# Attention and two mixture-of-experts layers: the table is entered one list later, the logits come in column fourths, and the second layer's rows are gathered before the earlier output

## The chip, the cores and the metric

One core of one Trainium2 chip runs the whole program in one launch. The metric is the device time of one execution in microseconds; it was 559.38 us (median of three runs).

## What is computed

Three parts follow each other; the first layer's capacity is 288 rows for an expert.

```python
# attention: q, k, v are 2 x 8 x 576 x 64, mask by blocks of 64
scores = where(block_i >= block_j, q @ k.T / 8, -1e9)
x = (softmax(scores) @ v)                         # then 1152 tokens x 512
# first layer: the best of 8 experts, at most 288 tokens each
e = argmax(x @ w_gate); gate = softmax(x @ w_gate)[e]
x = gate * (relu(x_e @ w1[e]) @ w2[e])            # 512 -> 1024 -> 512, 0 where not kept
# second layer: noisy choice of two of 8 experts
noisy = x @ w_gate + log1p(exp(x @ w_noise)) * noise
top2 = the two largest of noisy; weights = softmax over these two
out = sum over both of weight * (relu(x @ w1[e]) @ w2[e])
```

## The kernel before, in words

PE is TensorE, DVE VectorE, ACT ScalarE, POOL GpSimd, SP SyncE. The attention takes the first 141 us, the first layer's eight experts e0 to e7 about 141 to 334, the second layer the rest.

**Products.** A product in fp32 is made of three matmuls (`mm3`, L197 to L200): high part by high part, high by low, low by high. SP loads the weights as they are (`raw`), ACT makes the high part (L167), DVE the low one (L170). Tokens are handled in blocks of 128 rows, which indirect DMAs on POOL fetch: `xr` from x_d in the first layer (L1441), `g` in the second (L1418). PE transposes them (L1015), ACT and DVE split them (L1018, L1021).

**Order.** All work between the attention and the end is put into lists. A list is a `Flow` (L929): operations with an engine, a guessed duration and dependencies; `run` draws an order for every engine from weights and a random seed in `PAR` (L30). Each engine then goes through its own order and waits on semaphores. There is a list for each expert and arm, and at its end a branch. In the first layer the program holds two arms for each expert from e1 on: a short list (SMALL, one block of 128 rows or fewer) and a long one (LARGE, two blocks, and behind it a third block where the expert has more than 256 rows). In these data e1 to e4 take the short list, e5 to e7 the long one, and e6 also the third block. The list that carries over to the second layer is KNOWN (expert 0 of the second layer, from L1739), then comes `arm(e)` for e = 1 to 7 (kind SECOND), and `rest(e)` where an expert has over 256 rows.

**post (L1219).** When the first layer has finished a block of rows (`px`), `post` finds for each row its two experts of the second layer and the places in their lists. It runs in the next list: the last block of an expert is posted in the list of the next expert; in LARGE and in the third block another post runs within the list. There are twelve. Its steps:

- POOL: `place` (L1228 to L1233) and `send` (L1236), the scatter of the rows into x_d.
- PE transposes px (L1243), ACT copies it (`x2t`, L1247), and four matmuls make the logits (L1252): the rows are the stationary side, 16 columns of `wcat` (gate and noise) stream.
- ACT and DVE: exp, log, noise, the maximum and its index (L1256 to L1277), and M, the choice as ones and zeros (L1281).
- PE: the rank matmuls (L1286, L1288) count the rows of each expert; DVE picks the places (L1315 to L1325) and makes the weights v (L1303 to L1310).
- DVE: cells C (L1335), slots S (L1329) and C by v (L1340); PE: the table matmul (L1345, two of 144 columns); DVE adds the result to the table T (L1349).

T says which rows each expert of the second layer gathers. The table is the last matmul of most lists.

**Second layer.** `arm(e)` issues on POOL, in this order: the two fetches `prev` of what the output holds (L1577), then the next expert's gathers and the third block's (L1418), and at its end the scatters of the result (L1586), which have added the fetched rows (L1583). The fetches stand ahead of the list, where the loop at the end of the kernel calls them:

```python
for e in range(1, E):
    for blk in range(2):
        prev(G[e, blk][1], blk)
    arm(e)
```

Of the kernel before, what the change touches and what calls it, by code (L numbers as in the profile page):

```python
# [29 lines left out]
PAR = [dict(P=0.05, A=0.2, V=0.3, G=0.2, fit=0.52, late=0.548, dma=2.7, when=5.0, split=0, prep=1.8, post=1.85, last=2.5, seed=8387, noise=0.2),  # L30
       dict(P=0.2, A=0.2, V=0.2, G=0.1, fit=0, late=0.32, dma=2.44, when=10.0, split=6.3, prep=0, post=0.3, last=8.0, seed=5942, noise=0.2),
# [15 lines left out]
def attention_moe_moe2(ctx, tc, q, k, v, wg1, w1a, w2a, cap, wg2, wn2, noise, w1b, w2b, out):  # L47
    nc = tc.nc
# [44 lines left out]
    wcat = consts.tile([128, KD, 16], F32, name="wcat")  # L93
# [203 lines left out]
    with ExitStack() as actx:  # L297
# [69 lines left out]
        def gates(b):  # L367
            if b == B:
                nc.sync.dma_start(out=wcat[:, :, 0:8], in_=wg2.rearrange("(k p) e -> p k e", p=128))
# [556 lines left out]

    nc.vector.tensor_scalar(cum, ioe, float(NG), None, op0=OP.mult)
# [5 lines left out]
    class Flow:  # L933
# [4 lines left out]
        def __init__(self, kind=OTHER):  # L938
            self.kind, self.par, self.table = kind, PAR[kind], None
# [279 lines left out]
    def post(F, pd, n=128, deps=(), ranks=None, last=False, early=()):  # L1219
# [5 lines left out]
        def place():  # L1225
            fl = tl["fl"] = small.tile([128, 3], F32, name="fl")
            v = tl["v"] = small.tile([128, 2, 2], F32, name="v")
# [90 lines left out]
        def dest():  # L1318
            d = tl["di"] = small.tile([128, 3, 2], I32, name="di")
# [7 lines left out]
        def slots():  # L1327
            S2 = tl["S2"] = small.tile([128, 2, 128], F32, name="S2", bufs=1)
            nc.vector.tensor_tensor(S2[:n], tl["di"][:n, 1, :, None].to_broadcast([n, 2, 128]),  # L1329
                                    fslot[:n, None, :].to_broadcast([n, 2, 128]), op=OP.is_equal)  # L1330

        def cells():
            g = [n, 2, 8 * NG]
            C1 = tl["C1"] = small.tile([128, 2, 8 * NG], F32, name="C1", bufs=1)
            nc.vector.tensor_tensor(C1[:n], tl["di"][:n, 2, :, None].to_broadcast(g), iog[:n, None, :].to_broadcast(g), op=OP.is_equal)  # L1335

        def filled():
            g = [n, 2, 2, 8 * NG]
            C2 = tl["C2"] = small.tile([128, 2, 2, 8 * NG], F32, name="C2", bufs=1)
            nc.vector.tensor_tensor(C2[:n], tl["C1"][:n, :, None, :].to_broadcast(g), tl["v"][:n, :, :, None].to_broadcast(g), op=OP.mult)  # L1340

        def table(bank):
            tl["T"] = bank[:, 0:16 * NG]
            for j in range(2):
                nc.tensor.matmul(tl["T"], tl["S2"][:n, j], tl["C2"][:n, j].rearrange("p a g -> p (a g)"), start=(j == 0), stop=(j == 1))  # L1345

        def enter():
            c = T2[:, :, :, 0:NG]
            nc.vector.tensor_tensor(c, tl["T"].rearrange("p (a e g) -> p a e g", a=2, e=8), c, op=OP.add)  # L1349
# [25 lines left out]
        c = V(dest, [c])  # L1375
        c = V(parts, [c], 0.15)
        s2 = V(slots, [c, F.table], 0.33)
        c2 = V(cells, [c, F.table], 0.2)
        c2 = V(filled, [c2, w], 0.36)
# [436 lines left out]
```

## Time and profile before

| | |
|---|---|
| median of three runs | 559.38 us (557.72 to 559.82) |
| the profiled execution | 557.14 us, span 555.5 |
| PE busy | 517.0 us (93%) |
| DVE busy | 378.9 us (68%) |
| ACT busy | 294.1 us (53%) |
| POOL busy | 138.4 us (25%) |
| mean granted TensorE clock | 0.992 |
| DMA | 99.17 MB, mean 179 GB/s |

The profiled execution's own time is 1.6 us longer than its span; the median of the runs is 2.2 us above it. A busy share is an average over stages. Every view gives times from the start of the span. In a timeline, the bracket behind a row is the idle time of that engine before it and what ended it; rows start before their forerunner has ended where matmuls overlap, so the step between two of them is the difference of their starts.

### The profile page before, as it was taken

What the parts mean: (1) busy time and instruction counts of PE and PEld (TensorE: products, weight loads), DVE (VectorE), ACT (ScalarE), POOL (GpSimd) and SP (SyncE); (2) the same over time, 40 slices, a digit from 0 to 9 for tenths busy, and PEclk for the clock granted to TensorE, in tenths of its full rate; (3) what the DMA queues carried; (4) which work ended last, traced back from release to release, by engine and by line L of the source; (5) the groups of instructions that cost most, each with busy time, mean ns of one, the idle gap of its engine ahead of it and who ended that gap; (6) DMA issues with size and microseconds to landing.
All of it is one profiled execution on the core that took longest, in us unless ns stands there. A gap on an engine that the chain in (4) does not pass through costs nothing. (4 is left out here: it accounts for less than half of the span.)

```text
span 555.5 us, 10106 instructions
## 1 busy us (share of the span) xinstructions
PE 517.0 (93%) x3381; PEld 422.8 (76%) x3381; DVE 378.9 (68%) x1008; ACT 294.1 (53%) x580; POOL 138.4 (25%) x225
## 2 busy tenths in 40 slices
PE   3999999999869999999999999989999999969996
PEld 3778777878647776787976967888989886949794
DVE  7899988888548988757674678464848562917441
ACT  5888878871347687544533536252635442716130
POOL 3000000000462234405233133142513132514131
PEclk9999999999999999999999999999999999979999
DMA  6998896423458878754632442638658591545220
GB/s 136 221 240 229 220 230 188 123 77 109 137 176 290 265 240 296 232 189 138 206 133 64 170 137 71 226 125 284 221 205 280 188 327 48 187 180 165 86 66 35
DMA packets 71176, 99.17 MB, mean 179 GB/s; under 512 B 37130, under 2 KB 40586, under 8 KB 71088
## 3 DMA queue, kind: packets, MB, share of 16 engines
q1 hardware_dynamic: 63600, 83.16, 47.6%
q0 software_dynamic: 6432, 14.71, 8.4%
q8 instruction: 39, 0.64, 0.5%
q14 instruction: 49, 0.40, 0.2%
q10 hardware_dynamic: 1056, 0.26, 0.2%
HBM read 87.53 MB, written 12.25 MB: 180 GB/s over the span
## 5 line engine op out<-in xcount | busy, mean ns | idle before, releaser
L170 DVE TENSOR_TENSOR wl<-raw,wh 128x512 fp32r<-128x512 f32 x140 | 91.6, 685 | 12.0 <-ACT wh L167 11.6
L167 ACT ACTIVATE wh<-raw 128x1024 fp32r<-128x1024 f32 x70 | 71.1, 1052 | 20.1 <-PEq L1780 12.5
L170 DVE TENSOR_TENSOR both<-raw,both 128x512 fp32r<-128x512 f32 x100 | 66.0, 684 | 8.9 <-ACT both L167 8.4
L167 ACT ACTIVATE both<-raw 128x1024 fp32r<-128x1024 f32 x50 | 51.3, 1054 | 10.0 <-PEq L1780 8.3
L198 PE MATMUL h<-xh,wh 128*128 128x256 f32 (+1 forms) x184 | 52.9, 287 | 0.5
L199 PE MATMUL h<-xl,wh 128*128 128x256 f32 (+1 forms) x184 | 52.6, 286 | 0.0
L200 PE MATMUL h<-xh,wl 128*128 128x256 f32 (+1 forms) x184 | 52.5, 285 | 0.0
L1018 ACT ACTIVATE xh<-tp 128x512 fp32r<-128x512 f32 (+1 forms) x37 | 19.0, 536 | 59.0 <-PE tp L1015 57.3
L1021 DVE TENSOR_TENSOR xl<-tp,xh 128x512 fp32r<-128x512 f32 (+1 forms) x37 | 21.9, 610 | 35.3 <-ACT xh L1018 35.1
L1145 ACT ACTIVATE hh<-h 128x512 fp32r<-128x512 f32 (+1 forms) x46 | 24.1, 523 | 38.7 <-PE h L200 32.3
L1586 POOL DMA_INDIRECT out_dram<-o,T2i x16 | 18.5, 1156 | 96.9 <-DVE o L1583 94.8
L1148 DVE SCALAR_TENSOR_TENSOR hl<-h,hh 128x512 fp32r<-128x512 f32 (+1 forms) x46 | 27.5, 597 | 22.1 <-ACT hh L1145 18.0
L198 PE MATMUL h<-xh,both 128*128 128x256 f32 (+1 forms) x136 | 39.2, 288 | 2.7 <-DVE hl L1148 1.4
L199 PE MATMUL h<-xl,both 128*128 128x256 f32 (+1 forms) x136 | 39.0, 287 | 0.0
L200 PE MATMUL h<-xh,both 128*128 128x256 f32 (+1 forms) x136 | 38.8, 285 | 0.0
L198 PE MATMUL y<-wh,hh 128*128 128x512 f32 (+1 forms) x94 | 38.3, 407 | 0.0
L200 PE MATMUL y<-wh,hl 128*128 128x512 f32 (+1 forms) x94 | 37.1, 394 | 0.0
L199 PE MATMUL y<-wl,hh 128*128 128x512 f32 (+1 forms) x94 | 36.9, 393 | 0.0
L550 ACT ACTIVATE pt<-s,negmax 128x128 f32<-128x128 f32 (+3 forms) x64 | 33.4, 526 | 6.4 <-DVE negmax L537 5.1
L526 PE MATMUL s<-both 128*128 128x256 f32 (+2 forms) x128 | 33.1, 371 | 3.8 <-ACT both L468 2.5
L198 PEld LDWEIGHTS h<-xh,wh 128*128 128x128 f32 x184 | 34.7, 189 | 2.1 <-issue 1.6
L199 PEld LDWEIGHTS h<-xl,wh 128*128 128x128 f32 x184 | 34.6, 188 | 0.0
(295 smaller groups left out, 1297.9 us busy)
## 6 DMA issues: line engine op xcount, KB each, us to landing
raw<-in_moe_w_dram SPq DMA_DIRECT2D x120, 512.0 KB, 5.1
wf<-in_moe_w_dram SPq DMA_DIRECT2D x8, 512.0 KB, 5.8
out_dram<-zero SPq DMA_DIRECT2D x3, 768.0 KB, 5.5
both<-both SPq DMA_DIRECT2D x14, 160.0 KB, 2.6
raw<-in_q_dram SPq DMA_DIRECT2D x16, 128.0 KB, 4.2
vn<-in_v_dram SPq DMA_DIRECT2D x16, 128.0 KB, 2.6
both<-both SPq DMA_DIRECT2D x14, 144.0 KB, 3.3
raw<-in_k_dram SPq DMA_DIRECT2D x14, 128.0 KB, 4.7
```

What stands on the lines that cost most here:

```text
L167: nc.scalar.activation(h, t, AF.Copy)
L170: (nc.gpsimd if part == 3 else nc.vector).tensor_sub(l[:, c], t[:, c], h[:, c].bitcast(F32))
L198: nc.tensor.matmul(o, sh, mh, start=first, stop=False)
L199: nc.tensor.matmul(o, sh, ml, start=False, stop=False)
L200: nc.tensor.matmul(o, sl, mh, start=False, stop=last)
L526: nc.tensor.matmul(o, w[:, i, h, 128 * t:128 * t + 128], w[:, i + 2, h, 64 * h:64 * h + n], start=(i == 0), stop=(i == 1))
L550: nc.scalar.activation(o, i, AF.Exp, bias=negmax[:, pr, 2 * t + h:2 * t + h + 1], accum_out=ssum[b][:, t, 2 * p + h:2 * p + h + 1])
L1018: nc.scalar.activation(xh[:, :, c0:c0 + n], h["tp"][:, :, :n], AF.Copy)
L1021: nc.vector.tensor_tensor(xl[:, :, c0:c0 + n], h["tp"][:, :, :n], xh[:, :, c0:c0 + n].bitcast(F32), op=OP.subtract)
L1145: nc.scalar.activation(part(hfull[0], g - (KF - 2 * WHOLE) // per) if plain(g) else part(hh, g), of(g), AF.Relu)
L1148: nc.vector.scalar_tensor_tensor(part(hl, g), of(g), 0.0, part(hh, g).bitcast(F32), op0=OP.max, op1=OP.subtract)
L1586: ins = nc.gpsimd.indirect_dma_start(out=out, out_offset=_off(G[key][1][:n, 0:1]), in_=G[key, "o"][:n], in_offset=None, bounds_check=NT - ...
```

## The change

Five things are changed.

1. The steps from S and C to the addition into T leave `post` and become a function `enter`, with one buffer each for v, the places, S and C. A list now begins with the entering of the block that the list before has posted last. Only the posts that another post follows within the same list still enter at once (`now=True`), as does KNOWN's. The buffers begin as zeros, so that the first such entering, in e1's list, adds nothing: a thirteenth table. `place` and the picked places wait until the older ones have been read.
2. The logits: `wcat` is the stationary side, 32 columns (16 of them zero), 128 rows stream, and each of the four parts of the contraction goes to its own 32 partitions of PSUM. ACT copies that, and one matmul with `fold`, four stacked identities, sums the fourths.
3. SMALL and LARGE have other weights and seeds, so their orders are drawn anew.
4. The `prev`s of the second layer become entries of the list, and `to_out` depends on them.
5. Gathers that read T wait for the entering (`z`, `z0`).

```diff
-PAR = [dict(P=0.05, A=0.2, V=0.3, G=0.2, fit=0.52, late=0.548, dma=2.7, when=5.0, split=0, prep=1.8, post=1.85, last=2.5, seed=8387, noise=0.2),
+PAR = [dict(P=0.08, A=0.043, V=0.3693, G=0.1233, fit=0.097, late=0.6606, dma=1.5931, when=5.0, split=0, prep=2.0216, post=0.0021, last=10.4267, seed=4319, noise=0.7048),
...
-    wcat = consts.tile([128, KD, 16], F32, name="wcat")
+    wcat = consts.tile([128, KD, 32], F32, name="wcat")
+    fold = consts.tile([128, 16], F32, name="fold")
...
+    nc.gpsimd.tensor_tensor(fold, ident[:, 0:16], ident[:, 32:48], op=OP.add)
...
+    def enter(F, deps=(), early=(), tail="post"):
...
+        used = [F.table] if F.table else []
+        s2 = F.add("V", 0.33, slots, list(deps[:1]) + used)
+        c = F.add("V", 0.2, cells, list(deps[:1]) + used)
+        c2 = F.add("V", 0.36, filled, [c] + list(deps[1:]) + used)
+        t = F.table = F.add("P", 0.7, table, [s2, c2], take="sm")
+        F.entered = [s2, c2]
+        return F.add("V", 0.22, add, [t] + list(early), frees=t, tail=F.par[tail]), s2
...
         def logit(bank):
-            lg = tl["lg"] = bank[:, 0:16]
+            tl["lb"] = bank
             for kk in range(KD):
-                nc.tensor.matmul(lg[:n], tl["xt"][:, kk, :n], wcat[:, kk, :], start=(kk == 0), stop=(kk == KD - 1))
+                nc.tensor.matmul(bank[32 * kk:32 * kk + 32, 0:n], wcat[:, kk], tl["xt"][:, kk, :n], start=True, stop=True)
+
+        def fourths():
+            lq = tl["lq"] = yT.rearrange("p k n -> p (k n)")[:, 1024:1152]
+            nc.scalar.activation(lq[:, :n], tl["lb"][:, 0:n], AF.Copy)
+
+        def logits():
+            lg = tl["lg"] = tl["lb"][:, 128:144]
+            nc.tensor.matmul(lg[:n], tl["lq"][:, :n], fold, start=True, stop=True)
...
-        f = F.add("G", 0.8, place, deps)
+        f = F.add("G", 0.8, place, list(deps) + F.entered)
...
-        lg = F.add("P", 0.85, logit, [a], take="sm")
-        c = F.add("A", 0.1, ex, [lg])
+        lg = F.add("P", 0.45, logit, [a], take="sm")
+        c = F.add("A", 0.25, fourths, [lg])
+        c = F.add("P", 0.25, logits, [c])
+        c = F.add("A", 0.1, ex, [c])
...
+        if now:
+            z, s2 = enter(F, (c, w), early, "last" if last else "post")
...
-            nxt = post(F, first, last=True)[0] if first is not None else None
+            z = enter(F)[0] if first is not None else None
+            nxt = post(F, first, last=True, now=more)[0] if first is not None else None
...
-                d, _ = rows2(F, (0, 0), 0, 0, tis[0])
+                d, _ = rows2(F, (0, 0), 0, 0, tis[0], deps=[z])
...
-                    post(F, pend[2], deps=r, ranks=nxt)
+                    post(F, pend[2], deps=r, ranks=nxt, now=False)
...
-                _, z, _, tl = post(F, cur)
+                enter(F)
+                _, z, _, tl = post(F, cur, now=False)
...
-        blocks(F, E + e, xT[e % 2], 0, lambda y, blk, p, first: to_out(F, y, (e, blk), blk, p, first), done=done, apart=e + 1 == E)
+        before_ = [F.add("G", 1.04, lambda blk=blk: prev(G[e, blk][1], blk), after=3.5 if e + 1 < E else 0.0) for blk in range(2)]
+        blocks(F, E + e, xT[e % 2], 0, lambda y, blk, p, first: to_out(F, y, (e, blk), blk, p, first, deps=[before_[blk]]), done=done, apart=e + 1 == E)
...
-    d, i = rows2(F, (0, "early"), 0, 1, tis[1], deps=[d])
+    z0 = enter(F)[0]
+    d, i = rows2(F, (0, "early"), 0, 1, tis[1], deps=[d, z0])
...
-        for blk in range(2):
-            prev(G[e, blk][1], blk)
         arm(e)
```

Three places show how the instructions move. Line numbers of the change are its own: L1249 is the table, L1287 the transposes of px, L1296 the fourths, L1304 the fold, L1338 and L1340 the ranks, L1447 the gather, L1608 the prev, L1617 the scatter.

**POOL, the second layer's list of one expert**, before:

```order
L1577 DMA px_1732<-out_dram,T2i 128x512
L1577 DMA px_1733<-out_dram,T2i 128x512
L1418 DMA g_1740<-x_d,T2i 128x524
L1418 DMA g_1741<-x_d,T2i 128x524
L1418 DMA g_1742<-x_d,T2i 32x524
L1386 TENSOR_LOAD cnt_92
L1586 DMA out_dram<-o_6630,T2i 1152x512
L1586 DMA out_dram<-o_6631,T2i 1152x512
L1780 COMPARE_AND_BRANCH
```

and in the change:

```order
L1447 DMA g_1752<-x_d,T2i 128x524
L1447 DMA g_1753<-x_d,T2i 128x524
L1447 DMA g_1754<-x_d,T2i 32x524
L1608 DMA px_1744<-out_dram,T2i 128x512
L1608 DMA px_1745<-out_dram,T2i 128x512
L1415 TENSOR_LOAD cnt_93
L1617 DMA out_dram<-o_6546,T2i 1152x512
L1617 DMA out_dram<-o_6547,T2i 1152x512
L1811 COMPARE_AND_BRANCH
```

The two prevs move behind the three gathers, ahead of the scatters.

**PE, the end of e1's short list** (y is the second product, sm the small PSUM bank), before:

```order
L1288 MATMUL sm_1719<-M,before 128x8
L1015 MATMUL tp_1716<-ident,xr_1748 128x128 x4
L1080 MATMUL y_1712<-wh_96,hl 128x512
L184 MATMUL y_1712<-wf_1746,hf 128x512
L1015 MATMUL tp_1717<-ident,xr_1750 128x32 x4
L184 MATMUL y_1712<-wf_1746,hf 128x512
L1345 MATMUL sm_1718<-C_2881,S_2876 128x144 x2
L1537 UNCONDITIONAL_BRANCH
L1537 COMPARE_AND_BRANCH
L198 MATMUL h_1714<-xh_108,wh_97 128x288
```

and in the change, from the fold on:

```order
L1304 MATMUL sm_1720<-fold,yT 128x16
L1020 MATMUL tp_1719<-ident,xr_1760 128x128 x4
L1082 MATMUL y_1714<-wh_97,hh 128x512
L1082 MATMUL y_1714<-wl_103,hh 128x512
L1020 MATMUL tp_1718<-ident,xr_1761 128x128 x4
L1085 MATMUL y_1714<-wh_97,hl 128x512 x2
L185 MATMUL y_1714<-wf_1758,hf 128x512
L1020 MATMUL tp_1719<-ident,xr_1762 128x32 x4
L185 MATMUL y_1714<-wf_1758,hf 128x512
L1249 MATMUL sm_1721<-C_1738,S_1736 128x144 x2
L1338 LDWEIGHTS ones
L1338 MATMUL sm_1720<-cum,ones 128x8
```

The table comes ahead of the rank matmuls, and these, whose other three rows follow, are now the list's last work.

**PE, the beginning of KNOWN** (g and x of expert 0), before:

```order
L1537 UNCONDITIONAL_BRANCH
L1243 MATMUL tp_1716<-ident,px_1731 128x128 x4
L198 MATMUL h_1714<-wh_95,xh_108 128x512
L199 MATMUL h_1714<-wl_101,xh_108 128x512
L200 MATMUL h_1714<-wh_95,xl_109 128x512
L1252 MATMUL sm_1718<-wcat,x2t 128x16 x4
L198 MATMUL h_1714<-wh_96,xh_108 128x512
L199 MATMUL h_1714<-wl_102,xh_108 128x512
L200 MATMUL h_1714<-wh_96,xl_109 128x512
```

and in the change:

```order
L1568 UNCONDITIONAL_BRANCH
L1287 MATMUL tp_1718<-ident,px_1743 128x128 x4
L199 MATMUL h_1716<-wh_96,xh_109 128x512
L200 MATMUL h_1716<-wl_102,xh_109 128x512
L201 MATMUL h_1716<-wh_96,xl_110 128x512
L1249 MATMUL sm_1720<-C_1738,S_1736 128x144 x2
L1296 MATMUL sm_1721<-x2t,wcat 32x128 x4
L199 MATMUL h_1716<-wh_97,xh_109 128x512
L200 MATMUL h_1716<-wl_103,xh_109 128x512
L201 MATMUL h_1716<-wh_97,xl_110 128x512
L1304 MATMUL sm_1721<-fold,yT 128x16
```

The table of the last posted block stands between the first three matmuls and the logits; the fold follows three matmuls later.

## Rows read from the trace of the kernel before

**Rows 1.** What PE waited for, whole span: us in total, times, longest.

```profile
PE tp L1015 <- DMA g<-x_d,T2i: 5.0, 2, 4.6
...
PE sm L1345 <- DVE C L1340: 3.7, 8, 0.7
```

**Rows 2.** PE timeline, 488 to 503: start, us, engine line op [idle before <-releaser].

```profile
488.03 0.39 PE L200 MATMUL y<-both,hl 128*128 128x512 f32 x1
493.06 1.12 PE L1015 MATMUL tp<-ident,g 128*128 128x128 f32 x4 [4.64 <-DMA g<-x_d,T2i]
...
498.51 0.51 PE L198 MATMUL y<-both,hh 128*128 128x512 f32 x1
...
503.11 0.36 PE L198 MATMUL h<-xh,both 128*128 128x256 f32 x1
```

**Rows 3.** Timeline of POOL, 470 to 503 (same columns).

```profile
473.91 2.92 POOL L1586 DMA_INDIRECT out_dram<-o,T2i  x1 [5.11 <-DVE o L1583]
481.15 1.84 POOL L1577 DMA_INDIRECT px<-out_dram,T2i  x1 [4.31 <-DMA out_dram<-o,T2i]
...
485.08 1.46 POOL L1418 DMA_INDIRECT g<-x_d,T2i  x1 [0.32 <-issue]
...
488.15 0.94 POOL L1418 DMA_INDIRECT g<-x_d,T2i  x1 [0.30 <-issue]
```

**Rows 4.** Windows: busy PE, PEld, DVE, ACT, POOL; then PEclk, DMA share, GB/s.

```profile
488.00:493.00 5.00, 0.42 (x2) 0.00 (x0) 0.00 (x0) 0.00 (x0) 0.94 (x1) 0.84 0.95 374
493.00:498.00 5.00, 4.62 (x14) 3.28 (x14) 1.38 (x2) 1.20 (x2) 0.00 (x0) 0.50 0.07 27
```

**Rows 5.** PE timeline, 454 to 460, the same piece in another list.

```profile
455.18 0.40 PE L200 MATMUL y<-wh,hl 128*128 128x512 f32 x1
...
458.14 0.50 PE L198 MATMUL y<-wh,hh 128*128 128x512 f32 x1
```

**Rows 6.** Timeline of PE around the logits, 199.6 to 201.6.

```profile
200.26 0.96 PE L1252 MATMUL sm<-wcat,x2t 128*128 128x16 f32 x8
201.07 0.48 PE L198 MATMUL h<-wh,xh 128*128 128x512 f32 x1
```

**Rows 7.** Timeline of PE in the attention, 122 to 123.4.

```profile
122.66 0.42 PE L674 MATMUL tp<-xt,wblk 128*32 128x128 f32 x8
122.90 0.28 PE L675 MATMUL tp<-xt,wblk 128*32 128x64 f32 x2
```

**Rows 8.** Timeline of PE at a list's end, 176.5 to 180.

```profile
178.53 0.76 PE L1345 MATMUL sm<-C,S 128*128 128x144 f32 x4 [0.56 <-DVE C L1340]
179.05 0.47 PE L198 MATMUL h<-wh,xh 128*128 128x512 f32 x1
```

**Rows 9.** Timeline of DVE, a block's chain to M, 284 to 289.

```profile
285.51 0.17 DVE L1259 TENSOR_SCALAR a<-a 128x8 f32<-128x8 f32 x1
...
287.65 0.18 DVE L1281 TENSOR_TENSOR M<-ii,io 128x16 bf16<-128x16 uint32 x1
```

**Rows 10.** Timeline of DVE at the second layer's beginning, 331 to 344.

```profile
334.36 1.02 DVE L1558 MEMSET px<- 128x512 f32 x2 [0.98 <-DVEq L1529]
...
335.85 1.82 DVE L170 TENSOR_TENSOR both<-raw,both 128x512 fp32r<-128x512 f32 x3
...
341.36 0.30 DVE L1335 TENSOR_TENSOR C<-di,iog 128x144 f32<-128x144 int32 x1
...
341.98 0.45 DVE L1340 TENSOR_TENSOR C<-C,v 128x288 f32<-128x288 f32 x1
```

**Rows 11.** Timeline of PE at the second layer's beginning, 333 to 336.

```profile
334.61 0.40 PE L200 MATMUL h<-wh,xl 128*128 128x512 f32 x1
335.05 1.06 PE L1252 MATMUL sm<-wcat,x2t 128*128 128x16 f32 x8
```

**Rows 12.** POOL timeline, a scatter and the fetch behind it, 463 to 469.

```profile
464.28 1.00 POOL L1586 DMA_INDIRECT out_dram<-o,T2i  x1 [0.31 <-issue]
467.86 0.94 POOL L1577 DMA_INDIRECT pv<-out_dram,T2i  x1 [2.58 <-DMA out_dram<-o,T2i]
```

**Rows 13.** Timeline of POOL, a cast and its gather, 300 to 305.

```profile
302.42 0.19 POOL L1409 CAST ti<-T 128x1 int32<-128x1 f32 x1 [0.42 <-DVE T L1349]
303.36 1.25 POOL L1418 DMA_INDIRECT g<-x_d,ti  x1 [0.75 <-POOL ti L1409]
```

More of the change, by code (lines that the diff above doesn't have):

```diff
@@ L29 @@
 SMALL, LARGE, LARGE_R, SECOND, SECOND_R, KNOWN, OTHER, FIRST = range(8)
-PAR = [dict(P=0.05, A=0.2, V=0.3, G=0.2, fit=0.52, late=0.548, dma=2.7, when=5.0, split=0, prep=1.8, post=1.85, last=2.5, seed=8387, noise=0.2),
-       dict(P=0.2, A=0.2, V=0.2, G=0.1, fit=0, late=0.32, dma=2.44, when=10.0, split=6.3, prep=0, post=0.3, last=8.0, seed=5942, noise=0.2),
+PAR = [dict(P=0.08, A=0.043, V=0.3693, G=0.1233, fit=0.097, late=0.6606, dma=1.5931, when=5.0, split=0, prep=2.0216, post=0.0021, last=10.4267, seed=4319, noise=0.7048),
+       dict(P=0.4, A=0.0884, V=0.1582, G=0.051, fit=0, late=0.5397, dma=0.8093, when=10.0, split=7.6038, prep=1.8763, post=5.5326, last=0, seed=1201, noise=0.2003),
        dict(P=0.145, A=0.135, V=0.27, G=0.33, fit=0.087, late=0.3, dma=0, when=7.0, split=3.0, prep=0.6, post=2.587, last=13.6, seed=267, noise=0.7),
@@ L368, in gates @@
             if b == B:
+                nc.gpsimd.memset(wcat[:, :, 16:32], 0.0)
                 nc.sync.dma_start(out=wcat[:, :, 0:8], in_=wg2.rearrange("(k p) e -> p k e", p=128))
@@ L938, in __init__ @@
         def __init__(self, kind=OTHER):
-            self.kind, self.par, self.table = kind, PAR[kind], None
+            self.kind, self.par, self.table, self.entered = kind, PAR[kind], None, []
             self.random = random.Random(self.par["seed"])
@@ L1217, in to_pend, with slots, cells, filled @@
         return a, F.add("G", 0.2, cp, [p] + list(deps))
-    def post(F, pd, n=128, deps=(), ranks=None, last=False, early=()):
+    cv = small.tile([128, 2, 2], F32, name="v", bufs=1)
+    cdi = small.tile([128, 3, 2], I32, name="di", bufs=1)
+    cS = small.tile([128, 2, 128], F32, name="S2", bufs=1)
+    cC = [small.tile([128, 2, 8 * NG], F32, name="C1", bufs=1), small.tile([128, 2, 2, 8 * NG], F32, name="C2", bufs=1)]
+    nc.vector.memset(cv, 0.0)
+    nc.vector.memset(cdi, 0)
+    def enter(F, deps=(), early=(), tail="post"):
+        hold = {}
+        def slots():
+            nc.vector.tensor_tensor(cS, cdi[:, 1, :, None].to_broadcast([128, 2, 128]), fslot[:, None, :].to_broadcast([128, 2, 128]), op=OP.is_equal)
+        def cells():
+            g = [128, 2, 8 * NG]
+            nc.vector.tensor_tensor(cC[0], cdi[:, 2, :, None].to_broadcast(g), iog[:, None, :].to_broadcast(g), op=OP.is_equal)
+        def filled():
+            g = [128, 2, 2, 8 * NG]
+            nc.vector.tensor_tensor(cC[1], cC[0][:, :, None, :].to_broadcast(g), cv[:, :, :, None].to_broadcast(g), op=OP.mult)
+        def table(bank):
+            hold["T"] = bank[:, 0:16 * NG]
+            for j in range(2):
+                nc.tensor.matmul(hold["T"], cS[:, j], cC[1][:, j].rearrange("p a g -> p (a g)"), start=(j == 0), stop=(j == 1))
+        def add():
+            c = T2[:, :, :, 0:NG]
+            nc.vector.tensor_tensor(c, hold["T"].rearrange("p (a e g) -> p a e g", a=2, e=8), c, op=OP.add)
+        used = [F.table] if F.table else []
[5 more added lines that the diff above has]
+        return F.add("V", 0.22, add, [t] + list(early), frees=t, tail=F.par[tail]), s2
+    def post(F, pd, n=128, deps=(), ranks=None, last=False, early=(), now=True):
         px, pm, _ = pd
@@ L1226, in place @@
             fl = tl["fl"] = small.tile([128, 3], F32, name="fl")
[L1227 removed]
+            v = tl["v"] = cv
             nc.gpsimd.tensor_copy(v[:n, :, 0], pm[:n, 9:10].to_broadcast([n, 2]))
@@ L1318, in dest @@
         def dest():
-            d = tl["di"] = small.tile([128, 3, 2], I32, name="di")
+            d = tl["di"] = cdi
             nc.vector.tensor_copy(d[:n, 0], tl["fb"][:n, 0:2])
@@ L1374, in post @@
         c = F.add("V", 0.2, pick, [rk], frees=rk)
-        c = V(dest, [c])
+        c = V(dest, [c] + F.entered)
         c = V(parts, [c], 0.15)
-        s2 = V(slots, [c, F.table], 0.33)
-        c2 = V(cells, [c, F.table], 0.2)
-        c2 = V(filled, [c2, w], 0.36)
-        t = F.table = F.add("P", 0.5, table, [s2, c2], take="sm")
-        z = F.add("V", 0.22, enter, [t] + list(early), frees=t, tail=F.par["last" if last else "post"])
+        z = s2 = None
+        tl["read"] = [c, w]
+        if now:
+            z, s2 = enter(F, (c, w), early, "last" if last else "post")
         tl["sent"] = sent_
@@ L1518, in large @@
             begin(F)
-            done, nxt = beside(F, last)
+            done, nxt = beside(F, last, True)
             def fin(y, blk, p, first):
```

29 lines of the change are left out of this document (6 added, 23 removed).

## The prediction

> **What bounds the kernel now.** I read the page first: PE is busy in 93% of the span, every other engine in at most 68%. So a change pays only where PE's time gets shorter or where PE stands still. The second view is the list of what PE waited for. The reader is to see two entries there [rows 1]: 5.0 us on a gathered block of the second layer, nearly all in one place (4.6), and 3.7 us in eight waits on C, the last operand of the table matmul. The first is one wait, and a chain of one transfer stands behind it; the second is one short wait at the end of each first-layer list.
>
> Then the timeline of PE at the long wait [rows 2]: the matmul that begins at 488.03 is followed by the transposes of g only at 493.06. POOL's timeline of the same stretch [rows 3] says why: the gather was issued at 485.08, behind two fetches (px) that wait for the scatter of 473.91 to land in the output, which POOL sees at 481.15. The gather itself needs nothing of that scatter. Last, the granted clock [rows 4]: 0.84 in the idle stretch, and 0.50 in the 5 us after it, the lower of the two levels (1.2 instead of 2.4 GHz). So the wait costs more than its 4.6 us.
>
> **The second layer: prevs behind the gathers.** From the first `arm` on, PE, DVE, ACT and SP keep their order; POOL alone differs. In five of the six lists with a next gather PE never waits on it, so those cost and give nothing. For the sixth I compare the same piece of program at full clock. From one matmul before the transposes to the first matmul after the small transposes, the piece took 455.18 to 458.14 = 2.96 us [rows 5] and here 488.03 to 498.51 = 10.48 us [rows 2]. The difference is 7.5 us; the rest of the list (to 503.11) is nearly at full clock and gives at most 0.1. I take **-7.6**.
> This needs g early enough. POOL is free after the scatter's issue ends, 473.91 + 2.92 = 476.8, so the gather can start at about 477.1. The slowest landing seen is its own, 485.08 to 493.06 = 8.0 us, which would give 485.1, 3 us before PE asks at 488.3. The third gather, issued as far behind the first as now (485.08 to 488.15), lands by the same figure at 488.2, and PE asks for it later still. The prevs move to about 481 to 485 and nothing on POOL is queued behind them but the scatters of the list's end; their reader on DVE is there, past 495 in the new count. If the gather is still late by some part, that part is the loss; its bounds are 0 and -7.6.
>
> **The logits.** Before, four matmuls of 16 columns with the rows as weights took 200.26 to 201.07 = 0.81 us [rows 6]. The new form, four 32-column matmuls with 128 rows streaming, stands in the attention: 122.66 to 122.90 = 0.24 us for four [rows 7]. The fold is one matmul of the old kind, about 0.81/4 = 0.20. That is 0.37 saved per block, 4.4 us for twelve, if the two stood together. They don't: fourths and fold are two interruptions of a stream of three-part products. A matmul of 512 columns lasts 0.48 right behind the logits [rows 6] and 0.39 when it follows its like [rows 2], so each interruption costs some 0.08: 0.37 - 0.16 = 0.21, twelve times 2.5. I give 0.5 back for folds that wait for the new ACT copy: **-2.0**, bounds 0 and -4.4.
> The Trainium skill (TensorEngine Tiling (Array Packing), Performance Considerations) says that swapping the two operands and using four column tiles gives up to 4x when the moving side is 32 or less. By that the logits would take 0.81/4 = 0.20 and, with the fold, the saving would be 4.9 over twelve, the sum below -10.4; the same page (Key Properties) says that a change of tiling mode drains the engine, which speaks against doing it in the midst of other products. Rows 7 agree with the 4x for the four matmuls; no row prices a lone fold.
>
> **The table moved into the next list.** Before, the list ends with the table, which waits 0.56 us for C and then takes 178.53 to 179.05 = 0.52 [rows 8]. Afterwards its operands are made at the next list's start and the table has cover. But the list now ends with the rank matmuls, which wait for M. M comes 285.51 to 287.83 = 2.3 us after the first DVE step of the chain, about 2.7 after the logits [rows 9]. Between fold and rank PE has in the short list about what rows 5 hold plus the table, 2.96 + 0.52 = 3.5 us, and DVE puts splits of x into that stretch. So the new wait is near zero or some tenths, and what lay under the old wait (the branch, ACT's last copies) comes to light. Bounds for all eight: -3.7 (nothing takes their place) and 0 (all replaced). I take **-1.0**, nearer to 0, since the same chain only ends a step earlier.
> e1's list enters an empty table, a thirteenth: **+0.5** [rows 8].
>
> **Into the second layer.** In the known list the table stands behind the first transposes and three matmuls, where the logits stood. PE came there at 334.61 + 0.23 = 334.84 and then waited until 335.05 [rows 11]. The table needs C of the last post, and DVE reaches it only after three memsets, 334.36 to 335.85, and then needs 341.36 to 342.43 = 1.07 us for C, S and C2 (0.95 without the small step between) [rows 10]. So PE starts the table at 336.9: a wait of 2.1 in place of 0.2, **+1.9**; up to 2.6 if DVE leaves the arm late. Behind it on PE wait the logits and the stream of products; none of it can pass.
> In e7's list the gather of expert 0's first block now waits for the late table's addition into T. From the table's end I count 1.5 us to the gather's start (0.6 for the addition, then 302.42 to 303.36 from cast to issue, [rows 13]), then a landing: 464.28 to 467.86 = 3.6 us for a scatter in a quieter stretch [rows 12], 8.0 in the busiest [rows 2, 3]. PE has about 3.8 us of work in between (four groups of three, transposes and the logits; an estimate from rows 2 and 5), so the wait is 1.3 by the first and 5.7 by the second, and none if a gather lands in 2.3. I take **+0.7**, between none and the first.
> At nothing: the memsets of wcat and the fold's three additions (POOL waits 131 us for the attention there), two small memsets on DVE, the later `place` on POOL, which has a 25% load. If POOL were full, the sends would be late; they are not waited for within the list.
>
> **Sum.** -7.6 - 2.0 - 1.0 + 0.5 + 1.9 + 0.7 = -7.5. The profiled execution took 557.14 us (span 555.5), so its like would take 549.6. The median of the three runs, 559.38, is 2.24 above the profiled execution; the forecast in those terms is **551.9**.
>
> **Rivals.**
> More gain: the table waits vanish whole (-3.7 for -1.0) and the logits save their full 4.4 (for 2.0). -7.5 - 2.7 - 2.4 = -12.6, 546.8. For it: the lists are drawn anew with the new durations. Against: the chain to M is nearly as long as the work left to cover it.
> Less gain: the logits save nothing, the table waits are replaced, the known list waits 2.6 and e7's gather 1.3: -7.5 + 2.0 + 1.0 + 0.7 + 0.6 = -3.2, 556.2. For it: four places where a new wait is as likely as not. Against: all four at once.
> The gather stays late: then the -7.6 is missing and the sum is +0.1, 559.5. The condition is that its packets come through only once the weights are in: 374 GB/s at a DMA share of 0.95 while PE waits [rows 4]. Against it: an issue 8 us earlier has landed late only if the landing takes over 11 us, and none did.
> The Trainium skill (DMA: Bandwidth & Descriptors, Queues, rings and completion order) says that each DMA engine takes its queues in turn, packet by packet. By that the gather shares with the weights instead of standing behind them and the -7.6 comes; no row here shows single packets.
> Slower: the ranks end seven lists, and DVE has splits ahead of M. Three splits take 1.82 us [rows 10]; if each list's last rank waits so long, with nothing left on PE to cover it, that is 12.7 us against the 1.0 booked: 559.38 - 6.5 + 12.7 = 565.6. It decides against the change from (6.5 + 2.8)/7 = 1.3 us for each list on. Against it: the draw puts the chain's steps ahead of most splits on DVE.
>
> **How the numbers follow.** Forecast 0.62, more gain 0.13, less gain 0.14, gather late 0.07, slower 0.04. Two executions of this kernel differ by up to 0.4%, so I call 0.5% (2.8 us) the least that a measurement tells from no change. The forecast, more gain and most of less gain lie below 556.6: faster 0.87; the late gather and the rest: same 0.10; slower 0.03. The range goes from 546.6 to 556.4 and leaves out the late gather, the slower case and the tails.
>
> **What the profile after would show.** Right: PE's wait on g gone or under 1 us, the granted clock at 1.00 through that list, gathers before prevs on POOL at its start; logits near 0.24 plus a fold of 0.2; one new wait of about 2 us for C at the start of the known list; the waits for C at the ends of the lists gone, with a wait for M or nothing in their place. Wrong: PE still waiting on g there, a wait for M of over 1 us in most lists, or a clock of 0.50 in the first layer.

## The result, and the profile after

The changed kernel took **562.35 us** (median of 16 runs, 559.03 to 564.43); the kernel before took 557.08 in the same comparison (16 runs). The ratio is 1.0084, 95% interval 1.0063 to 1.0105: **slower**, where 551.9 was forecast. A second comparison of the same two programs gave 560.68 against 558.20 and 1.0033 [0.9997, 1.0070] (e12 below), so the loss is some tenths of a per cent up to one. A ratio is taken over the fast runs (in e12 two of eleven, over 1.5% above its fastest, are left out) and differs by up to 0.2% from the quotient of the medians. The three runs of before that were shown (559.38) lay high; against the 557.08 of the comparison the forecast would have been 549.6.

The profiled execution of after took 560.19 us, span 558.4; before it was 557.14, span 555.5. What PE waited for in after, whole span (us in total, times, longest), answers to [rows 1]:

```profile
PE tp L1020 <- DMA xr<-x_d,T: 3.7, 2, 2.4
PE h L199 <- ACT wh L168: 3.0, 1, 3.0
...
PE tp L1017 <- DVE hl L1070: 2.4, 1, 2.4
PE sm L1249 <- DVE C L1244: 1.9, 1, 1.9
...
PE tp L1020 <- DMA g<-x_d,ti: 0.6, 1, 0.6
```

The 4.6 on the gathered block of the second layer and the eight waits on C at the lists' ends are gone. New are 3.0 at the start of a first-layer list, and 2.4 and 1.9 in the known list. By stages, before to after in us: attention 141.28 to 142.12; first layer 192.40 to 193.74; **known list 30.29 to 38.73**; second layer from its first `arm` 191.53 to 183.81. These two executions differ by 2.9 us, the medians by 5.3.

**Second layer.** The same piece as in [rows 2 to 4], PE's windows and POOL's timeline of after (everything stands 10.6 us later there):

```profile
485.00:490.00 5.00, 5.00 (x45) 5.00 (x44) 5.00 (x9) 4.98 (x7) 4.59 (x2) 1.00 0.52 164
490.00:495.00 5.00, 5.00 (x38) 4.71 (x37) 5.00 (x10) 2.44 (x4) 4.50 (x2) 1.00 0.92 293
495.00:500.00 5.00, 5.00 (x28) 4.21 (x27) 1.19 (x2) 0.55 (x2) 2.78 (x3) 1.00 0.90 296
```

```profile
484.44 2.93 POOL L1617 DMA_INDIRECT out_dram<-o,T2i  x1 [5.09 <-DVE o L1614]
487.67 2.23 POOL L1447 DMA_INDIRECT g<-x_d,T2i  x1 [0.30 <-issue]
...
495.50 1.58 POOL L1608 DMA_INDIRECT px<-out_dram,T2i  x1 [0.31 <-issue]
```

The gather is issued right behind the scatter and the previous rows behind it; PE is full and its clock at 1.00.

**Logits.** PE's timeline at one block (start, us, line) answers to [rows 6]:

```profile
173.88 0.42 PE L1296 MATMUL sm<-x2t,wcat 128*32 128x128 f32 x8
174.24 0.50 PE L1085 MATMUL y<-wh,hl 128*128 128x512 f32 x1
...
175.03 0.29 PE L1304 MATMUL sm<-fold,yT 128*128 128x16 f32 x2
175.17 0.53 PE L1020 MATMUL tp<-ident,xr 128*128 128x128 f32 x3
```

0.36 for the fourths and 0.14 for the fold, 0.50 in place of 0.81.

**The known list.** PE's timeline, answering to [rows 11], then its windows (busy PE, PEld, DVE, ACT, POOL; granted clock, DMA share, GB/s):

```profile
336.79 0.40 PE L201 MATMUL h<-wh,xl 128*128 128x512 f32 x1
339.12 1.33 PE L1249 MATMUL sm<-C,S 128*128 128x144 f32 x4 [1.93 <-DVE C L1244]
340.38 0.66 PE L1296 MATMUL sm<-x2t,wcat 128*32 128x128 f32 x8
...
350.85 0.72 PE L1082 MATMUL y<-both,hh 128*128 128x512 f32 x2
354.01 0.49 PE L1017 MATMUL tp<-ident,g 128*128 128x128 f32 x2 [2.45 <-DVE hl L1070]
```

```profile
338.00:340.00 2.00, 0.88 (x3) 0.88 (x4) 1.67 (x5) 0.12 (x1) 0.70 (x2) 0.50 0.04 8
340.00:342.00 2.00, 2.00 (x13) 1.15 (x13) 1.51 (x4) 0.85 (x2) 1.54 (x3) 0.50 0.00 0
342.00:344.00 2.00, 2.00 (x7) 1.71 (x6) 1.22 (x5) 1.42 (x3) 0.63 (x2) 0.50 0.70 175
344.00:346.00 2.00, 2.00 (x9) 1.53 (x9) 1.42 (x9) 1.04 (x4) 0.00 (x0) 0.84 0.97 364
...
354.00:356.00 2.00, 1.99 (x13) 1.99 (x14) 2.00 (x4) 0.00 (x0) 0.65 (x1) 0.72 0.27 52
356.00:358.00 2.00, 2.00 (x8) 1.81 (x8) 0.65 (x2) 0.60 (x1) 1.01 (x1) 0.50 0.20 82
```

The wait for C is there, 1.93. Behind it the clock stands at 0.50 until 344 and at 0.84 until 346: of the 6 us from 340 to 346, (2 + 2) x 0.5 + 2 x 0.16 = 2.3 are lost. At 354 comes a second wait, of 2.45, and behind it again 2 x 0.28 + 2 x 0.50 = 1.6. The four together are 8.3 of the 8.4 us by which this list grew. DVE's timeline shows what the second wait is:

```profile
351.61 0.16 DVE L1748 TENSOR_TENSOR flag<-worst 128x1 int32<-128x1 f32 x1
351.69 0.31 DVE L1253 TENSOR_TENSOR T<-sm,T 128x144 f32<-128x144 f32 x1
353.16 0.20 DVE L1455 CAST T2i<-T 128x80 int32<-128x80 f32 x1 [1.16 <-issue]
353.28 0.68 DVE L1070 TENSOR_TENSOR hl<-tp,hh 128x512 fp32r<-128x512 f32 x1
```

Between T and the cast stands the load of `flag` into a register (L1784, a load that every engine executes, at 352.1 on PE and 352.8 on DVE). In before it stood behind the cast, hl and PE's transposes; the list as drawn now puts it ahead of all three, so PE waits for hl behind it.

**The first layer.** The 3.0 us are put down to ACT's wh, which had long been there. PE's timeline, and the rows of the branch at the third list's beginning (L1568: engine, operation, ns, start):

```profile
179.80 0.19 PE L1340 MATMUL sm<-M,before 128*128 128x8 bf16 x2
182.96 0.47 PE L199 MATMUL h<-wh,xh 128*128 128x512 f32 x1 [2.97 <-ACT wh L168]
```

```profile
L1568 ACTq COMPARE_BRANCH  x1: 45/45/45, 179.5 to 179.5; - x1
L1568 PEldq COMPARE_BRANCH  x1: 3292/3292/3292, 179.5 to 179.5; - x1
```

PE's sequencer stands 3.29 us in the branch; in before the same branch takes 0.35:

```profile
L1537 PEldq COMPARE_BRANCH  x1: 347/347/347, 178.5 to 178.5; - x1
```

The list of transfers of 180.4 to 180.5 holds one packet, of 16 KB, of a queue that the profile calls "instruction":

```profile
q8 instruction: 1, 0.02, 59.5%
```

That packet takes 0.95 us, and the branch ends 1.4 us after it. Behind the branch (184 to 188) the clock is 0.57.

### The profile page after: what moved, and what is told of

Same layout as the page of the kernel before. It is cut to its first block, busy times and chain, and to the rows that moved or that the text cites. A ratio compares the mean times of both kernels' runs of the same rounds, so it can differ in the third digit from the quotient of the medians.

```text
span 558.4 us, 10200 instructions
## 1 busy us (share of the span) xinstructions
PE 519.8 (93%) x3409; PEld 422.2 (76%) x3409; DVE 381.5 (68%) x1014; ACT 296.7 (53%) x592; POOL 146.1 (26%) x229
## 5 line engine op out<-in xcount | busy, mean ns | idle before, releaser
L168 ACT ACTIVATE wh<-raw 128x1024 fp32r<-128x1024 f32 x70 | 70.7, 1051 | 19.5 <-PEq L1811 12.6
L1617 POOL DMA_INDIRECT out_dram<-o,T2i x16 | 18.4, 1152 | 100.0 <-DVE o L1614 97.8
L552 ACT ACTIVATE pt<-s,negmax 128x128 f32<-128x128 f32 (+3 forms) x64 | 33.3, 525 | 6.3 <-DVE negmax L539 5.2
L1466 POOL MEMSET xr<- 128x524 f32 x3 | 1.5, 548 | 131.1 <-DVE T1f L813 131.1
```

The lines of the kernel that those rows point to most:

```text
L168: nc.scalar.activation(h, t, AF.Copy)
L552: nc.scalar.activation(o, i, AF.Exp, bias=negmax[:, pr, 2 * t + h:2 * t + h + 1], accum_out=ssum[b][:, t, 2 * p + h:2 * p + h + 1])
L1617: ins = nc.gpsimd.indirect_dma_start(out=out, out_offset=_off(G[key][1][:n, 0:1]), in_=G[key, "o"][:n], in_offset=None, bounds_check=NT - ...
```

## The experiments

The theory at the start: the known list loses through a wait for C that was forecast and a wait behind the flag that was not; the first layer loses through something else. The rival: the rest of the change costs everywhere a little, through the lower clock. Ratios are to before, runs on the same chip. "Under the change" is against the 562.35 above, which was measured in another round; against the second measurement of the change, 560.68, each such difference is 1.7 us smaller.

**e1: previous rows alone.** Before, with this edit only:

```diff
+        before_ = [F.add("G", 1.04, lambda blk=blk: prev(G[e, blk][1], blk), after=...) for blk in range(2)]
-        blocks(..., lambda y, blk, p, first: to_out(F, y, (e, blk), blk, p, first), ...)
+        blocks(..., lambda y, blk, p, first: to_out(F, y, (e, blk), blk, p, first, deps=[before_[blk]]), ...)
...
-            prev(G[e, blk][1], blk)
```

> The kernel before with one part of the change: the prevs of the second layer behind the gathers. Theory (the stall of 4.64 us and the half clock behind it were in most executions of the kernel before, and go): 7.6 us less than before, a ratio of 0.986, and from the beginning of the second expert's list to the end 184 us instead of 191.5. Rival (the stall was an accident of the profiled execution): within 2 us of before.

550.22 us, 0.9879 [0.9841, 0.9918]; later once more (e11) 550.13, 0.9862 [0.9839, 0.9885]. From the first `arm` to the end 183.8 us, as in after. The forecast gain of 7.6 is there, and this one edit is faster than before.

**e2: no table carried into the known list.** After, with the last expert's blocks entering the table at once, as before:

```diff
-            nxt = post(F, first, last=True, now=more)[0] ...
+            nxt = post(F, first, last=True, now=more or e + 1 == E)[0] ...
...
-    z0 = enter(F)[0]
-    d, i = rows2(F, (0, "early"), 0, 1, tis[1], deps=[d, z0])
+    d, i = rows2(F, (0, "early"), 0, 1, tis[1], deps=[d])
```

> The changed kernel, but e7's blocks enter the table at once, so that no table is carried into the list that begins the second layer. Theory (the carried table makes that list 38.7 us long instead of 30.3, by its own wait, by the half clock that follows and by the flag load that it moves ahead): about 8.4 us less than the changed kernel, 554 us, and that list 30 to 31 us long. Rival (the loss comes from the redrawn lists of the first layer, and the second layer's list only inherits their clock): over 559 us, and the list still over 36 us.

556.85 us, 0.9970 [0.9943, 0.9997]: 5.5 under the change; the known list takes 33.3 us. That lies between the two: the waits of 1.9 for C and 2.4 for hl are gone from the list, but PE stands 1.8 us in it for nothing that the profile shows ("issue"). In e10, which has the same edit, it does not, and the list takes 31.4.

**e3: the flag late.** After, with `guess` drawn without its 12 us of lead:

```diff
-    F.add("P", 0.5, guess, [c], tail=12.0)
+    F.add("P", 0.5, guess, [c], tail=0.0)
```

> The changed kernel with one edit: the load of the flag that steers the branch for left-over rows gets no weight, so that it stands behind the transposes on PE and behind the cast of T on DVE, as it did before the change. Theory (DVE and PE stood 1.2 and 2.4 us at that load, and the half clock of 354 to 358 us follows from it): 3 to 5 us less than the changed kernel, 557.5 to 559.5; the first wait for C (1.9 us) and the half clock behind it stay. Rival (PE waited there for the late hl itself, whatever stands ahead of it): within 1 us of the changed kernel.

557.56 us, 0.9998 [0.9972, 1.0023]: 4.8 under the change. The known list takes 35.3; the wait of 1.9 stays, that for hl is gone. At the list's end PE loses 0.5 more than in the change (0.84 for 0.30), at a branch that e9 comes back to. Without it the edit gives 4.0 in this list, and 4.4 over before are left. So both waits cost about what the windows said, 4.0 and 4.2 with the clock behind them. The 4.8 of the medians need not be this list alone: in the two profiles e3's first layer, which the edit leaves as it is, is 4.0 us shorter (189.8) and its attention 1.6 longer.

**e4: the old lists.** After with before's planner settings for the two kinds of first-layer list:

```diff
-PAR = [dict(P=0.08, A=0.043, ... post=0.0021, last=10.4267, seed=4319, noise=0.7048),
+PAR = [dict(P=0.05, A=0.2, ... post=1.85, last=2.5, seed=8387, noise=0.2),
...
```

> The changed kernel with the weights and seeds of the short and long lists as they were before. Theory (the wait of 3.0 us for the split weights at the beginning of e2's list comes from the redrawn order on ACT): that wait under 0.5 us, about 3 us less than the changed kernel, 559, while the list that begins the second layer stays at 38 us. Rival (it comes from the rank as the list's last work, under any draw): the wait is there again, at 2 us or more, at one or more of the four short lists' ends.

562.03 us, 1.0087 [1.0057, 1.0117], no different from the change. The wait is there under the old draw too, but as the branch, which takes 4.48 us here. So the new draw is not what makes the loss; a gain of about the 1.2 us by which this branch is longer could hide behind it.

**e5, e8: logits in fourths with the table where it was.** e5 is before with the fourths and the fold only; e8 adds e1's edit.

```diff
-                nc.tensor.matmul(lg[:n], tl["xt"][:, kk, :n], wcat[:, kk, :], ...)
+                nc.tensor.matmul(bank[32 * kk:32 * kk + 32, 0:n], wcat[:, kk], tl["xt"][:, kk, :n], ...)
+            nc.scalar.activation(lq[:, :n], tl["lb"][:, 0:n], AF.Copy)
+            nc.tensor.matmul(lg[:n], tl["lq"][:, :n], fold, start=True, stop=True)
```

> The kernel before with one part of the change: the logits in column fourths with their fold, drawn with the weights and seeds of before. Theory (0.17 to 0.2 us less for each of twelve blocks): 1 to 2.5 us less than before, a ratio of 0.9955 to 0.998; the four matmuls take 0.24 us and the fold 0.14 where it follows its like. Rival (the longer chain of three more steps gives it back at the lists' ends): no difference, and the waits of the table for C grow from 3.7 us to 5 or more.

> The kernel before with two parts of the change, the prevs behind the gathers and the logits in fourths; the table stays where it was. Theory (the two gains stand in different stages and add): the sum of both parts alone, 548 to 549.5 us, a ratio of about 0.984. Rival (the logits give nothing once they are not at the end of a wait): 550, as the prevs alone.

e5: 567.95 us, 1.0199 [1.0172, 1.0226]. e8: 560.79, 1.0044 [1.0011, 1.0077], its executions from 555.1 to 564.8. So the fourths alone gain nothing; they cost 10.7 us against before and 10.6 against e1 (9.2 by the ratios). PE's waits of e8 up to the known list, then those of e1:

```profile
PE sm L1358 <- DVE C L1353: 10.0, 8, 2.0
```

```profile
PE sm L1345 <- DVE C L1340: 3.8, 8, 0.7
```

The fourths shorten PE's work and lengthen the chain behind it (copy, fold, then all the steps to C). With the table still at the list's end, the eight waits grow by 6.2 us; the mean clock is 0.983 for e1's 0.997, with stretches of 10 us at 0.75 to 0.90 in the first layer (in e1 one, at 0.86). In e5 this is not the whole price: from the second list's first transposes to the third's it takes 23.9 us for before's 17.1, and PE's branch in that stretch 3.98 us; in e8, with the branch at 0.42, it takes 18.2. From the third list's transposes to the known list, where neither has a long branch, e5 takes 156.2 us for before's 151.8, and e8 157.6 for e1's 152.1: 4.4 and 5.5 more.

**e7: the table carried, nothing else.** Before with `enter` split from `post` and run in the next list:

```diff
+            z = enter(F)[0] if first is not None else None
-            nxt = post(F, first, last=True)[0] ...
+            nxt = post(F, first, last=True, now=more)[0] ...
```

> The kernel before with one part of the change: the table is entered one list later, drawn with the weights and seeds of before, the logits and the prevs as before. Theory (the carried table costs 8 us in the list that begins the second layer and gives less than 1.5 in the first layer's lists): 5 to 9 us more than before, and that list at 37 us or longer. Rival (the carried table alone is harmless, and its loss comes with the fourths and the new draw): within 2 us of before, and that list at 31 to 33 us.

569.81 us, 1.0226 [1.0194, 1.0258]. PE's longest wait of e7 between 141 and 378, and the known list at 36.1:

```profile
PE tp L1015 <- DMA g<-x_d,ti: 5.9, 1, 5.9
```

A long branch is in this price too, at another list. Into the fifth list PE's sequencer takes 2.85 us (0.86 in before), and from the fourth list's transposes to the fifth's it is 19.7 us for before's 17.1.

Carrying alone costs 12.6 us, the fourths alone 10.7, the previous rows give 7.5; the sum would be +15.8, and the change has +5.3 (e4, with the planner settings of e5 and e7, +4.3). The first two belong together: in the change no list of the first layer ends with a wait for C, and e7's 5.9 is 0.6. Why that gather's wait shrinks was not tried apart.

**e6: code moved.** After with 64 more matmuls in the second list's third block, which is never entered, so nothing that is executed differs; PE's code behind it lies 64 instructions later (the code behind the branch to the third list at 1594 in place of 1530).

```diff
-                w = F.add("P", 1.6, lambda b: busy(b, 7), ends, take="h")
+                w = F.add("P", 1.6, lambda b: busy(b, 71 if e == 1 else 7), ends, take="h")
```

> The changed kernel with 64 more matmuls in an arm that these data never enter (e1's third block): no instruction that runs is changed, PE's code behind it only stands further on. Theory (the 3.3 us that PE's sequencer spends in the branch from e1's to e2's list come from where the code of that list stands): that branch under 0.9 us, as the others, and 3 to 5 us less than the changed kernel, 557.5 to 559.5, unless another branch becomes slow. Rival (it comes from the rank and not the table standing last in the list, or from the new order of the splits): the branch is again at 2 us or more and the time within 1 us of the changed kernel.

556.04 us, 0.9986 [0.9962, 1.0010], 6.3 under the change (4.6 by its second measurement):

```profile
L1568 PEldq COMPARE_BRANCH  x1: 352/352/352, 180.3 to 180.3; - x1
```

From the second list's first transposes to the third's it takes 15.9 us, against 19.7 in the change's first profile and 19.0 in its second (e12). All nine profiles of the change and of its variants that share these two lists agree: 15.9 to 16.0 us with this branch at 0.35 (e6, e9, e10), 17.8 with it at 2.15 (e3, e14), 19.0 to 20.5 with it at 3.3 (the change, e2, e12, e15). So the branch costs 1.8 us at 2.15 and 3.0 to 4.5 at 3.3. What e6 gains beyond that these profiles do not place; its first list is even the slowest of the nine. The next branch takes 0.72 in e6, for 0.37.

**e9, e10, e11: what is left without the losses.** e9 is e6 and e3 together, e10 is e6 and e2, e11 repeats e1.

> The changed kernel with two edits that each came out level with before when made alone: 64 more matmuls in the first expert's third block, which is not entered (e6: 556.04, 6.3 us under the change), and the flag's load drawn late (e3: 557.56, 4.8 us under). Theory, two separate losses at two places (PE's branch between the second and third list, and the wait of 2.45 us behind the flag in the second layer's beginning): the gains add, 562.3 - 6.3 - 4.8 = 551.2 us; the branch takes about .35 us, and KNOWN lasts about 35 us. Rival, both gains come from one thing, TensorE's granted clock over the whole span or the addresses of all code behind the edit: together no more than the larger, about 556 us. Faster than before by about 1% under the first, level under the second.

> The changed kernel with the 64 matmuls of e6 and with the last expert's blocks entered at once (e2: 556.85, 5.5 us under the change). If the losses are separate: 562.3 - 6.3 - 5.5 = 550.5 us, the branch at about .35 us, KNOWN at about 33 us. If they share one cause: about 556 us. If the table's late entry into the second layer's beginning costs anything that the flag does not, this run ends below e9.

> The kernel of e1 again (before, with only the previous rows' loads put behind the gathers), beside e9 and e10 on one chip: 550.2 us again, 0.988 of before. If the rest of the change (fourths, the table carried, the new lists) is worth anything once its two losses are taken away, e9 or e10 ends below this one; if it is worth nothing, they end level with it or above.

e9: 555.56 us, 0.9969 [0.9944, 0.9994]. e10: **548.91**, 0.9853 [0.9823, 0.9883]. e11: 550.13. In e10 the gains add (550.5 expected, 552.2 if counted from 560.68). So the rival of the start, a little cost everywhere, is out: with two places mended the loss is gone. In e9 the gains do not add: there the branch over the second layer's left-over work takes 3.93 us, with a 16 KB packet of the instruction queue at 364.0 to 364.5, inside it:

```profile
L1804 PEldq COMPARE_BRANCH  x1: 3933/3933/3933, 363.1 to 363.1; - x1
```

PE stands 1.28 us there and 2.16 soon behind it, and from 371 to 375 the clock is 0.57. The branch takes 3.47 in e3, where PE loses only 0.5 by it, and 0.35 in after. In e3 and e9 the flag, whose load also marks that branch for PE beforehand (L1785), is loaded on PE less than 1 us ahead of it, in after 18 us ahead. That the late mark makes the branch long fits these three, but e4, with the early flag, has 2.26; it was not tried apart.

**e12 to e15: does the place of the code decide?** e12 is the change once more; e13 is e1 with 7 unexecuted matmuls (branch at 1530, as in the change); e14 and e15 are the change with 256 and 8 (1786 and 1538).

> The changed kernel once more, beside e13 to e15 on one chip. If the long branch of PE between the second and the third list belongs to the program (3.29 us in its profile, 3.35 and 2.16 in e2 and e3, which have the same code up to there), this execution has it again, at 2 us or more, and the time is 562 us; if it comes by chance of the execution, it is about .35 us here, and e6's gain of 6.3 us is not explained by it.

> e1's kernel (550.2 us) with 7 more matmuls in the first expert's third block, which is not entered: the code behind that branch then lies at the same place in PE's program as in the changed kernel (instruction 1530; 1523 in e1). If the place of the code alone makes the branch long: 2 to 4.5 us of branch between the second and the third list, and 553 to 556 us. If the place is not what matters: branch .35 us, 550 us.

> The changed kernel with 256 more matmuls in that block that is not entered: all code behind it lies 256 instructions later (the code behind the branch at 1786 in place of 1530), in the same place within a block of 256 as in the changed kernel. If the place within a block of 256 instructions decides (a block is what the Trainium skill's page Runtime: NRT & Kernel Launch, section Instruction fetch mechanics, says is fetched at a time), the branch is long again, 2 us or more, and the time 562 us. If any shift of the code cures it: .35 us and 556 us, as e6 with 64.

> The changed kernel with 8 more matmuls in that block (the code behind the branch at 1538). If the long branch needs its code to lie just ahead of a multiple of 256 (1530 of 1536 in the change), it is gone: .35 us and about 556 us. If it hangs on a place farther off, or on chance: 2 us or more, 560 to 562 us.

| | us | ratio | branch, us |
|---|---|---|---|
| e12 | 560.68 | 1.0033 [0.9997, 1.0070] | 3.33 |
| e13 | 550.86 | 0.9875 [0.9839, 0.9911] | 0.35 |
| e14 | 561.10 | 1.0064 [1.0036, 1.0093] | 2.15 |
| e15 | 560.72 | 1.0031 [1.0005, 1.0057] | 3.34 |

The long branch comes back with the program (e12) and goes with a shift of 64, but not with one of 8 or 256, and the same place in e1's program is harmless. So it is neither an accident of one execution nor the place alone.

What the branch waits for, the seventeen profiles show together. Behind the first 130 us PE has 24 branches of over 0.6 us in them, at five places, and every one ends 1.2 to 1.6 us after a 16 KB packet of the instruction queue has landed. At the branch to the third list such a packet starts 0.9 to 1.5 us after the branch where that takes 3.3 to 4.5 us, and 0.4 us before it where it takes 2.15 (e3, e14); in the nine profiles where it is short, none is under way while it lasts. So PE waits there for a packet of code. What decides whether the code is there in time is open: e5 and e8, with the same code up to there, had 3.98 and 0.42.

The times of e14 and e15 say less than the last column. In their profiles the first layer takes 188.3 and 189.0 us, no more than in e6, and the known list 41.6 and 41.2 for the change's 38.7 and 38.9, with a wait of 2.6 and 2.2 on POOL's `cum` that the change does not have.

## Why the prediction was wrong

The step that failed is the price of what the change adds: +1.9 for the known list, where 8.4 came, and nothing for PE's branch in the first layer, which took 3.3 us. The term that carried the gain was right.

- **"Prevs behind the gathers, -7.6": right.** -7.7 in after, -7.5 in e1's time. The half clock was part of the stall and went with it.
- **"Into the second layer, +1.9": right as a wait, wrong as a price.** The wait was 1.93 for the 2.1 forecast. Its price is 4.2, because the clock stays at 0.50 behind it. The text had used exactly this in [rows 4] for the gain, and not for the new wait. With e2's edit most of the list's growth goes (33.3).
- **The flag: a step that was not counted.** I looked at what the change adds to the known list, and not at which instructions the new draw moves there. The load of the flag went ahead of the cast, hl and the transposes: 2.45 us, 4.0 with the clock (e3: 4.0 in this list). This moves no arithmetic, so it costs nothing in a sum of operations.
- **"Logits, -2.0": right only together with the carried table.** PE's own saving is 0.81 - 0.50 = 0.31 a block, near the 0.37 without interruptions (the fourths took 0.36 for the 0.24 of [rows 7], the fold 0.14 for 0.20). But I set it off against PE alone. In a list that ends by waiting for this chain the saving is lost and the chain's growth is added: waits 6.2 us longer, the kernel 9 to 11 us (e5, e8; in e5 with a long branch). The other sum in the text, with 4.9 saved in place of 2.0, is -10.4 and not below it.
- **"List ends, -1.0": too little.** All eight waits for C went (-3.7), and no wait for M came in their place. The first list varies by itself (last section), so I count from the second list's first transposes to the known list. Where the branch is short this takes 164.8 (e6), 166.8 (e9) and 168.4 (e10) us, 166.7 on average, against 168.9 in before, 169.3 in e1 and 169.2 in e11; the terms of the first layer summed to -1.8. In the six profiles with the long branch it takes 167.7 to 171.2, on average 169.2. So there is a gain of about the forecast's size, and the branch takes it back; single profiles spread as much as the gain.
- **"e7's gather, +0.7": right**, 0.6.
- **The branch, 0 in the sum: wrong.** 3.3 us for 0.35, in both profiles of this program. The Trainium skill (Runtime: NRT & Kernel Launch, Instruction fetch mechanics) says that a taken branch whose target has not been fetched forces a fetch of its block, in 16 KiB, before execution goes on. The trace agrees: in after, e2, e4, e5, e12 and e15 a 16 KB packet of the instruction queue starts 0.9 to 1.5 us after the long branch begins, and the branch ends 1.4 us after it has landed. In e6 such a packet starts 1.0 us behind the start of the branch too, but that branch was over after 0.35 and waited for none. No row of before that I read showed a long branch; its trace holds one of 0.86, into the fifth list at 211.9, and e11 has 1.61 there.
- **The rival "slower"** named waits for M at seven list ends. None came; the loss has other places. The chance of slower, 0.03, was too low for a change that draws every list anew and moves most of PE's code.

By stages the forecast was -1.8, +1.9, -7.6 for the first layer, the known list and the second; measured were +1.3, +8.4, -7.7, and 0.8 in the attention. That is 2.9 us between the two profiled executions; the other 2.4 of the 5.3 between the medians no profile places.

The version that beats both kernels is e10 (548.91), level with the previous rows alone (550.13 on the same chip). So the fourths and the carried table are worth at most about 1 us once their losses are gone, within what these runs can tell.

## What to carry to other kernels

Price a new wait with the clock behind it: here 1.9 and 2.45 us of standing cost 4.2 and 4.0, though a wait of 3.0 cost no clock in one execution (e12, below). Where a change draws an order anew, go through the few instructions that every engine executes (register loads, branches) before the arithmetic, since whatever they overtake or hold up is in no sum. And make one part at a time: here one edit held the whole gain, two others cost about 10 us each alone, long branches included, and little together.

## What the runs showed that was not expected

- The same conditional branch on PE took 0.34 to 0.42 us in some programs and 2.2 to 4.5 us in others, ending 1.4 to 1.6 us after an instruction packet had landed; 64 instructions that are never executed took 3 us off it and 4.6 to 6.3 us off the kernel.
- The clock's level follows single waits: 0.50 to 0.57 for about 4 us behind the waits of 2.97 and 1.93 us in after, and 0.72 and 0.50 behind that of 2.45. It does not always: in e12 PE stands 3.01 us at the same branch, until 181.0, and from there to 189 the clock is at 1.00. Over the span the mean was 0.980 in after, 0.992 in before, 0.997 in e1 and e10; 558.4 x 0.020 = 11.2 us against 555.5 x 0.008 = 4.4 is an upper bound (idle stretches count in it) that would hold more than the whole loss.
- In the first list a half clock comes and goes between executions of code that is alike up to there: from its start to the second list's first transposes it took 20.7 us in e12, 24.1 in the change's first profile and 25.0 in e6. Single profiles differ by that much without any edit. So does the attention: 141.8 us in e1 and 143.9 in e11, the same program.
